# Loading group 0, the weights and half of group 1 as one series of cast DMAs

## The chip, the cores and the metric

The kernel runs on one core of a Trainium2 chip. The metric is the device time of one execution in microseconds (us). A profiled execution adds a trace; its span is the time from the first to the last instruction. Engines are named as in the profile: PE (TensorE matmul), PEld (weight load), DVE (VectorE), ACT (ScalarE), POOL (GpSimd), SP (SyncE).

Every run is labelled fast unless it is more than 1.5% above the fastest run of the same kernel.

## The reference

```python
# x: (8, 4224, 192); weight: (8, 7); w_in: (192, 1024); A_log: (512,); w_out: (512, 192), all float32
w = softmax(weight)                      # 8 heads of 24 channels, 7 taps
x = causal_conv(x, w)                    # out[s] = sum_k w[h, k] * x[s - 6 + k], zero before each sequence
proj = x @ w_in
val, gate = proj[..., :512], proj[..., 512:]
h = exp(A_log)[0] * h + val[:, t]        # scan over the 4224 positions of each sequence
out = (silu(gate) * h) @ w_out
```

## The kernel before

The 33,792 rows are two streams of 16,896, worked side by side. A group is 16 tiles of 96 rows per stream, a quarter is 4 tiles. The conv is a matmul against a banded matrix `tb`; its output is transposed (by PE for the first half of group 0, by the DMA crossbar afterwards) into `xc`. A step projects 512 positions of each stream for one of 4 channel blocks: `pv` (values, scanned on VectorE) and `pg` (gates, SiLU on ScalarE), then GpSimd multiplies. From step 9 on, output matmuls run as well.

The head of the program, shortened and with comments added:

```python
WARM, WARM2 = 8, 6
...
ws = ...; nc.sync.dma_start(ws, weight.unsqueeze(0))
for st in range(2):                       # quarter 0, fp32, cast later on an engine
    load_raw((nc.scalar, nc.sync)[st], 0, st, 0)
nc.gpsimd.dma_start(al, moe_A_log.rearrange("(c p) -> p c", p=P))
for st in range(2):                       # quarter 1, cast in the DMA
    load_cast(0, st, QT, HT)
nc.sync.dma_start(w1r, moe_w_in[0:D1, :]) # fp32 weights, cast on GpSimd
for m in range(0, D2, DI):
    for st in range(2):
        nc.sync.dma_start(w2r[st * D2R : st * D2R + D2R, m : m + DI], moe_w_in[D1:D, m : m + DI])
...
warm(pw, WARM)                            # matmuls on zeros
...                                       # softmax and banded matrix
warm(pw, WARM2)
...
for st in range(2):
    cast_raw((nc.scalar, nc.gpsimd)[st], 0, st)
for st in range(2):
    load_cast(0, st, HT, HT + QT)         # quarter 2
```

w_in has 192 rows; `w1` holds the first 128. `w2` holds the last 64 twice, on partitions 0 to 63 and 64 to 127, one copy for each stream. The start of the pipeline and the first steps:

```python
conv_main(None, pair(ps_g, "pg"), 0, True)    # quarter 0
conv_main(None, pair(ps_v, "pv"), 1, True)    # quarter 1
...
warm(misc()[:, 0:N], 4)
for m in range(0, D2, DI):
    nc.gpsimd.tensor_copy(w1[:, m : m + DI], w1r[:, m : m + DI])
    nc.gpsimd.tensor_copy(w2[:, m : m + DI], w2r[:, m : m + DI])
for st in range(2):
    load_cast(0, st, HT + QT, GT)             # quarter 3
load_cast(1, 0, 0, HT)
trans_pe(0)
phase(-1)                                     # first projection
conv_main(nc.scalar, misc(), 2); trans_main(2)
for s in range(NSTEP):
    ...                                       # scan(s), phase(s), mul(nc.gpsimd, s)
    if gr == 0:
        ...
        if s < 3:
            load_cast(1, (s + 1) % 2, (s + 1) // 2 * HT, (s + 1) // 2 * HT + HT)
        if s == 3:
            nc.gpsimd.dma_start(wout, ...)
        if s in (5, 7):
            load_raw(nc.sync, 2, s // 7)
        if s in (6, 8):
            load_cast(2, s // 8, QT, GT)      # 504 KB each
    ...
    if s in todo:                             # 5, 6, 7, 8, 10, 12, ...: conv and crossbar transpose
        conv(todo[s])
```

At step 7 the mixed channels of group 1 (`ymix`) are convolved; their crossbar transpose is issued on SP at the end of that stretch, and step 11 needs it for its last projection matmuls.

## Time and profile before

| | before |
|---|---|
| time, the first 3 runs | 343.25 to 345.82 us, median 345.59 |
| span of the profiled run | 343.5 us |
| first scan | 17.62 us |
| scan of step 2 / 8 / 12 / 20 | 22.34 / 36.17 / 45.54 / 64.95 us |
| transpose of ymix for step 11 | issued 38.32, landed 6.4 us later, PE waited 0.2 us |

The lines behind this are in the prediction. The waits list puts down a wait to what came last, and gives total, count and longest.

### The profile page before, as it was taken

How to read it: one execution, taken by the hardware profiler on the slowest of the kernel's cores; microseconds unless marked ns; L12 is line 12 of the kernel's file. 1: busy time of each engine (PE TensorE's matmuls, PEld its weight loads, DVE VectorE, ACT ScalarE, POOL GpSimd, SP SyncE). 2: the span in 40 equal slices, each digit the busy share in tenths (PEclk: the TensorE clock that was granted, in tenths of full speed). 3: DMA queues.
4: the chain of work that ended last, by engine and by line, in shares of the span. 5: the costliest groups of instructions: out<-in, count | busy, mean ns of one | idle time of the engine just before them, and what ended most of it. 6: DMA issues, size and time to landing. Idle time of an engine off the chain costs nothing.

```text
span 343.5 us, 7220 instructions
## 1 busy us (share of the span) xinstructions
PE 330.3 (96%) x2604; PEld 179.2 (52%) x2605; DVE 324.3 (94%) x311; ACT 271.1 (79%) x431; POOL 305.8 (89%) x176
## 2 busy tenths in 40 slices
PE   6698999999999999999999999999999999999994
PEld 2433455555545555555545555455555555556444
DVE  3399999999999999999999999999999999999994
ACT  4367888978987888798888789789888888777663
POOL 7569999999989998998998999899899988888882
PEclk9899999999999999999999999999999999999999
DMA  8959999998998999999799799989979954545235
GB/s 190 143 66 183 157 190 248 200 168 203 167 221 145 160 169 239 165 192 188 181 213 149 184 167 158 231 185 176 196 176 168 209 138 126 139 105 149 92 112 169
DMA packets 126839, 58.53 MB, mean 170 GB/s; under 512 B 84338, under 2 KB 126290, under 8 KB 126802
## 3 DMA queue, kind: packets, MB, share of 16 engines
q1 hardware_dynamic: 94722, 45.64, 66.1%
q0 software_dynamic: 31472, 11.90, 31.8%
q10 hardware_dynamic: 608, 0.53, 0.5%
q8 instruction: 20, 0.33, 0.4%
q14 instruction: 17, 0.14, 0.2%
HBM read 31.70 MB, written 25.95 MB: 168 GB/s over the span
## 4 chain that ended last, share of the span: by engine, by line
PE 87%; DVE 4%; DMA 4%; issue 1%; ACT 1%; POOL 0%; DVEq 0%; POOLq 0%; ACTq 0%
PE pm L444 26%; PE pv L361 15%; PE pg L361 15%; PE pg L369 11%; PE pm L257 9%; PE pv L369 8%; DVE h L411 4%; DMA xb<-in_x_dram 3%; DMA xc<-ymix 2%; ACT sg L393 1%; PE pv L257 1%; PE pm L178 1%; PE pg L444 0%; PE pv L444 0%; POOL al L156 0%
## 5 line engine op out<-in xcount | busy, mean ns | idle before, releaser
L411 DVE TENSOR_TENSOR_SCAN h<-av,h,pv 128x512 bf16<-128x512 f32 (+3 forms) x256 | 294.9, 1210 | 2.9 <-issue 1.9
L429 POOL TENSOR_TENSOR y<-sg,h 128x1024 bf16<-128x1024 bf16 x130 | 273.3, 2124 | 27.0 <-ACT sg L393 25.7
L393 ACT ACTIVATE sg<-pg 128x512 bf16<-128x512 f32 x262 | 142.2, 594 | 30.9 <-PE pg L369 29.5
L444 PEld LDWEIGHTS <-y 128*128 128x128 bf16 x1056 | 83.9, 98 | 26.8 <-issue 26.8
L444 PE MATMUL pm<-wout,y 128*128 128x192 bf16 x1024 | 95.6, 247 | 0.0
L361 PE MATMUL pv<-xc,w 128*128 128x512 bf16 x265 | 80.5, 379 | 2.4 <-DVE h L411 2.2
L361 PE MATMUL pg<-xc,w 128*128 128x512 bf16 x262 | 78.3, 378 | 0.3
L468 ACT COPY osb<-pm 128x768 f32<-128x768 f32 x64 | 51.3, 802 | 24.7 <-ACT sg L393 23.2
L361 PEld LDWEIGHTS <-w 128*128 128x128 bf16 x528 | 46.9, 98 | 37.0 <-issue 7.1
L369 PE MATMUL pg<-xc,w 64*128 64x512 bf16 x262 | 51.1, 386 | 0.0
L369 PE MATMUL pv<-xc,w 64*128 64x512 bf16 x266 | 50.5, 376 | 0.2 <-DMA xc<-ymix 0.2
L257 PEld LDWEIGHTS <-tb 112*96 112x96 bf16 x440 | 32.8, 124 | 31.4 <-issue 28.8
L369 PEld LDWEIGHTS <-w 64*128 64x128 bf16 x528 | 15.3, 94 | 57.9 <-issue 57.9
L105 ACT CAST ymain<-pm 96x1024 bf16<-96x1024 f32 x42 | 42.3, 1007 | 1.0 <-PE pm L257 0.8
L257 PE MATMUL pm<-xb,tb 112*96 112x192 bf16 (+2 forms) x420 | 41.4, 237 | 0.0
L121 POOL DMA_DIRECT2D xb<-in_x_dram x28 | 25.3, 905 | 0.0
L411 DVE TENSOR_TENSOR_SCAN h<-av,pv 128x512 bf16<-128x512 f32 (+3 forms) x32 | 24.9, 795 | 0.4 <-PE pv L369 0.4
L105 ACT CAST ymix<-pm 96x1024 bf16<-96x1024 f32 x20 | 20.1, 1007 | 0.0
L105 ACT CAST xb<-xraw 112x768 bf16<-112x768 f32 x19 | 15.8, 833 | 0.0
L178 PE MATMUL pg<-wm 128*128 128x512 bf16 x14 | 5.1, 524 | 1.7 <-DVE wm L171 1.7
L178 PEld LDWEIGHTS <-wm 128*128 128x128 bf16 x18 | 2.1, 129 | 4.4 <-issue 2.2
L257 PE MATMUL pv<-xb,tb 112*96 112x192 bf16 (+2 forms) x13 | 1.9, 327 | 2.2 <-DMA xb<-in_x_dram 2.2
(61 smaller groups left out, 38.7 us busy)
## 6 DMA issues: line engine op xcount, KB each, us to landing
out_dram<-osb SPq DMA_DIRECT2D x65, 384.0 KB, 3.6
xb<-in_x_dram POOLq DMA_DIRECT2D x18, 504.0 KB, 8.8
xraw<-in_x_dram SPq DMA_DIRECT2D x18, 336.0 KB, 4.1
xb<-in_x_dram POOLq DMA_DIRECT2D x4, 336.0 KB, 6.1
xc<-ymain SPq DMA_TRANSPOSE x84, 4.7
xb<-in_x_dram POOLq DMA_DIRECT2D x6, 168.0 KB, 5.7
w1r<-in_moe_w_in_dram SPq DMA_DIRECT2D x1, 512.0 KB, 6.2
w2r<-in_moe_w_in_dram SPq DMA_DIRECT2D x4, 128.0 KB, 6.9
```

Source lines behind the costliest of these rows:

```text
L105: eng.copy(o, i)
L121: eng.dma_start(t[:, b0 : a1 - a0, :], dataclasses.replace(xf, offset=xf.offset + (row + b0 * M) * D, ap=[[D, K], [M * D, a1 - a0 - b0], [ ...
L178: nc.tensor.matmul(ps, wm[:, 0:P], wm, start=True, stop=True)
L257: nc.tensor.matmul(pc[:, :, :, lo - lo0 : hi - lo0], tb[:, h, :], xbs[g][:, :, a : a + QT, lo:hi], start=(lo == lo0), stop=(hi == hi0), sk ...
L361: nc.tensor.matmul(ps[st], w1[:, m * P : (m + 1) * P], xc[:, st, t], start=True, stop=False)
L369: nc.tensor.matmul(ps[st], w2[r, m * P : (m + 1) * P], xc[r, 2, t], start=False, stop=True)
L393: nc.scalar.activation(sg[:, st * N : st * N + N], pgs[st], Act.Silu)
L411: nc.vector.tensor_tensor_scan(h[:, o + lo : o + hi], av[:, c : c + 1].to_broadcast([P, hi - lo]), pv[st][:, lo:hi], initial=0.0 if lo in ...
L429: eng.tensor_mul(y, sg, h)
L444: nc.tensor.matmul(pk[b // 2][:, b % 2, :], y[:, b : N : NB] if w >= NOUT - 2 else y[:, b * P : b * P + P], wout[:, c, :], start=(b % 2 == ...
L468: nc.scalar.copy(osb.rearrange("p (k b) d -> p k (b d)", k=2), po)
```

## The change

The intent was to bring everything that the start needs in order of need, through one queue, with the cast done by the DMA, and to have no such load in flight while the first crossbar transposes run. Core of the diff, shortened and with comments added:

```diff
-WARM = 8
-WARM2 = 6
+WARM = 6
+WARM2 = 4
...
+    x0 = singles.tile([K, D], FP32, name="x0")       # the very first tile, cast on VectorE
+    nc.scalar.dma_start(x0[HB:K, :], xf[0:M, :])
+    nc.sync.dma_start(al, moe_A_log.rearrange("(c p) -> p c", p=P))
     for st in range(2):
-        load_raw((nc.scalar, nc.sync)[st], 0, st, 0)
-    nc.gpsimd.dma_start(al, ...)
-    ...                                              # w1r, w2r: fp32 loads on SP
+        load_cast(0, st, 0, QT)
...
+    for st in range(2):
+        load_cast(0, st, QT, HT)
+    nc.gpsimd.dma_start(w1, moe_w_in[0:D1, :])
+    nc.gpsimd.dma_start(
+        w2,
+        dataclasses.replace(
+            moe_w_in, offset=moe_w_in.offset + D1 * D2, ap=[[0, 2], [D2, D2R], [1, D2]]
+        ),
+    )
...
+    for q in (2, 3):
+        for st in range(2):
+            load_cast(0, st, q * QT, q * QT + QT)
+    for st in range(2):
+        load_cast(1, st, 0, HT)
...
-    warm(misc()[:, 0:N], 4)
-    ...                                              # four weight casts on GpSimd, later loads
+    warm(misc()[:, 0:N], 2)
...
-            if s < 3:
-                load_cast(1, ...)
-            if s == 3:
+            if s in (3, 4):
+                load_cast(1, s - 3, HT, GT)
+            if s == 5:
                 nc.gpsimd.dma_start(wout, ...)
```

Here `ap` lists (step, count) pairs: the source of w2 starts with a pair of step 0, so it reads the 64 rows twice.

More of the change, by code (lines that the diff above doesn't have):

```diff
@@ L115, in load @@
         row = st * TS + (g * GT + a0) * M - HB
-        b0 = 0
-        if g == 0 and a0 == 0:
-            nc.vector.memset(t[0:HB, 0, :], 0.0)
-            eng.dma_start(t[HB:K, 0, :], xf[row + HB : row + K, :])
-            b0 = 1
+        b0 = 1 if row < 0 else 0
         eng.dma_start(
@@ L152 @@
     nc.sync.dma_start(ws, weight.unsqueeze(0))
+    x0 = singles.tile([K, D], FP32, name="x0")
+    nc.scalar.dma_start(x0[HB:K, :], xf[0:M, :])
+    al = singles.tile([P, NC], FP32, name="al")
+    nc.sync.dma_start(al, moe_A_log.rearrange("(c p) -> p c", p=P))
     for st in range(2):
-        load_raw((nc.scalar, nc.sync)[st], 0, st, 0)
-    al = singles.tile([P, NC], FP32, name="al")
-    nc.gpsimd.dma_start(al, moe_A_log.rearrange("(c p) -> p c", p=P))
-    for st in range(2):
-        load_cast(0, st, QT, HT)
-    w1 = singles.tile([P, D2], BF16, name="w1")
-    w2 = singles.tile([P, D2], BF16, name="w2")
-    w1r = singles.tile([P, D2], FP32, name="w1r")
-    w2r = singles.tile([P, D2], FP32, name="w2r")
-    nc.sync.dma_start(w1r, moe_w_in[0:D1, :])
-    for m in range(0, D2, DI):
-        for st in range(2):
-            nc.sync.dma_start(
-                w2r[st * D2R : st * D2R + D2R, m : m + DI], moe_w_in[D1:D, m : m + DI]
-            )
+        load_cast(0, st, 0, QT)
+    nc.vector.memset(x0[0:HB, :], 0.0)
     wm = singles.tile([P, N], BF16, name="wm")
@@ L198 @@
         )
+    for st in range(2):
+        load_cast(0, st, QT, HT)
+    w1 = singles.tile([P, D2], BF16, name="w1")
+    w2 = singles.tile([P, D2], BF16, name="w2")
+    nc.gpsimd.dma_start(w1, moe_w_in[0:D1, :])
[5 more added lines that the diff above has]
+    )
     ident = singles.tile([M, M], BF16, name="ident")
     make_identity(nc, ident)
+    for q in (2, 3):
[3 more added lines that the diff above has]
+        load_cast(1, st, 0, HT)
     wmax = singles.tile([1, H], FP32, name="wmax")
@@ L240 @@
     nc.scalar.activation(quiet, av[:, 0:1], Act.Silu)
-    for st in range(2):
-        cast_raw((nc.scalar, nc.gpsimd)[st], 0, st)
-    for st in range(2):
-        load_cast(0, st, HT, HT + QT)
+    nc.vector.tensor_copy(xbs[0][:, 0, 0, :], x0)
+    zero_halos(0, 0)
     ymain = {}
@@ L490 @@
         )
-    warm(misc()[:, 0:N], 4)
-    for m in range(0, D2, DI):
-        nc.gpsimd.tensor_copy(w1[:, m : m + DI], w1r[:, m : m + DI])
-        nc.gpsimd.tensor_copy(w2[:, m : m + DI], w2r[:, m : m + DI])
-    for st in range(2):
-        load_cast(0, st, HT + QT, GT)
-    load_cast(1, 0, 0, HT)
+    warm(misc()[:, 0:N], 2)
     trans_pe(0)
@@ L535 @@
                 trans_main(3)
-            if s < 3:
-                load_cast(1, (s + 1) % 2, (s + 1) // 2 * HT, (s + 1) // 2 * HT + HT)
-            if s == 3:
+            if s in (3, 4):
+                load_cast(1, s - 3, HT, GT)
+            if s == 5:
                 nc.gpsimd.dma_start(wout, moe_w_out.rearrange("(c p) m -> p c m", p=P))
```

## The prediction

> **What bounds the kernel now.** I read the page first, then the chain of waits, then the busy time by stretch, then the DMA windows of the first 45 us. The page's busy row and first chain row:
>
> ```profile
> PE 330.3 (96%) x2604; PEld 179.2 (52%) x2605; DVE 324.3 (94%) x311; ACT 271.1 (79%) x431; POOL 305.8 (89%) x176
> PE 87%; DVE 4%; DMA 4%; issue 1%; ACT 1%; POOL 0%; DVEq 0%; POOLq 0%; ACTq 0%
> ```
>
> PE and VectorE are both nearly full, so most of the span is closed to this change, which touches loads of the first two groups only. The chain in order of time shows the head:
>
> ```profile
> 3.02 8.75 DMA xb<-in_x_dram
> 11.77 0.04 issue
> 11.81 1.85 PE pv L257 x13
> 13.66 1.72 PE pm L178 x4
> 15.38 0.04 issue
> 15.42 0.50 PE pm L324 x8
> 15.92 0.68 PE pg L324 x16
> 16.60 0.58 PE pv L361 x2
> 17.19 0.37 PE pv L369 x2
> 17.56 0.01 DVEq L411
> 17.57 0.05 issue
> 17.62 4.55 DVE h L411 x4
> ```
>
> Columns are start, length, what. The load of quarter 1 of group 0 (issued at 3.02) lands at 11.77; then 13 conv matmuls, 4 warm-up matmuls, the PE transposes and the first projection follow, and the first scan starts at 17.62. From there two stages follow. In steps 0 to 8 VectorE is the bound: by stretch, it is busy 22.28 of the 22.28 us from 17.62 to 39.90, PE only 19.84, and the waits list has PE waiting 2.2 us for scans. From step 9, when the output matmuls join, PE is back to back: 16 output matmuls begin every 4.82 us (45.20, 50.02, 54.84), that is every two steps, against four scans of 1.2 us. So **the time of the first scan, plus any later stall that exceeds the small slack, is what the change can move**; 345.6 us is the reference.
>
> The DMA stage table of the head:
>
> ```profile
> 5.20:8.58 3.38, 1.94 (x14) 0.93 (x13) 1.04 (x2) 2.16 (x4) 2.39 (x4) 1.00 1.12 273
> 8.58:12.00 3.42, 0.82 (x9) 0.70 (x10) 0.69 (x1) 0.83 (x2) 1.96 (x4) 1.00 1.43 216
> 12.00:15.40 3.40, 3.37 (x17) 2.05 (x16) 1.37 (x2) 1.16 (x2) 2.38 (x4) 0.50 0.72 75
> ```
>
> After the stretch come its length, the busy times of PE, PEld, DVE, ACT and POOL, the granted clock, the DMA share and GB/s. The reader is to see two things: the DMA engines are full (1.12, 1.43) while PE waits, and the stretch after the idle one runs PE at clock 0.50. That is why 13 matmuls take 1.85 us and each warm-up matmul 0.43.
>
> **What the Trainium skill says.** (1) "DMA: Bandwidth & Descriptors", section "Issuing engines are not separate DMA queues": loads from all issuers share the same 16 DMA engines and interleave. The trace agrees: quarter 1 took 8.7 us while 1.0 MB of weights were moved beside it; the same size took 3.6 and 3.8 us from about 12 us on. (2) Same page, "Rules for kernel authors": a leading zero-stride broadcast of c copies confines a DMA to at most c engines; the page also names an exception in which a GpSimd direct copy keeps 16. The new load of w2 has just this source (2 copies of 64 rows). No run here shows which holds. (3) "TensorE: Matmul & The Clock Gate", Part 1: the clock is set from activity in free-running windows of about 3.41 us. The trace agrees (0.50 for 3.4 us after 0.82 us of work in the window before).
>
> **The change part by part.**
>
> Removed: the fp32 staging of group 0's first quarter (648 KB over two hardware queues), 1.0 MB of fp32 weights in flight beside quarter 1, six casts (0.82 on POOL, 0.82 on ACT, 4 x 0.61 on POOL), the 0.95 us POOL issue of A_log, and 2 + 2 + 2 warm-up matmuls. Of the last only the third pair lies on the chain: 2 x 0.43 at half clock, 2 x 0.25 at full.
>
> Added: casts inside the DMA, a 192-column copy on VectorE (under 0.3 us, beside the load) and a small ScalarE memzero.
>
> Moved: the first cast DMA issues at about 1.4, each issue 0.70. Quarter 0: two issues, to 2.8; band mask, 0.8 to 3.6; quarter 1, to 5.0; w1 and w2, to about 6.5; quarters 2 and 3 and half of group 1, to about 11.5 (0.70 for a quarter, 0.86 for a half).
>
> How fast does this series flow? Between 10.5 and 12 us the DMA window counts 746 cast rows of 768 B in 1.5 us, 498 rows per us. Quarters 0 and 1 are 784 + 896 = 1,680 rows, so 3.4 us of flow. The start is slower: packets begin 0.6 us after the end of an issue, and from 24 us, after one, some 1.3 us run at 50 instead of 190 GB/s; I allow 1 us for that and 0.8 us more because A_log's first packets of this queue came later still (4.0, issue ended 2.31). Last row of quarter 1: 2.1 + 0.6 + 1.8 + 3.4 = 7.9; landing about 0.9 later (the 336 KB load at 22.56: its 896th row is counted at about 27.0, it landed at 27.66; others 1.1), so **8.8 instead of 11.77**. Quarter 0 lands near 7, ready about when the mask product, the copy and the memzero are.
>
> From landing to first scan: 13 matmuls at full clock 1.2 (7 took 0.63 at 8.93), two warm-ups 0.5, then 15.42 to 17.62 unchanged, 2.2: first scan at 12.7. At half clock it is 1.85 + 0.86 + 2.2, 13.7. I take 13.0, a gain of **4.6 us**. The weights must be there by 11.7 and 12.2: w1 and w2 are 512 KB each at about 370 GB/s (the window 5.5 to 6.5, nearly all w1, moved 368), 1.4 us each, so their data end at 9.3 and 10.7 and land by 11.6 if w2 uses 16 engines: just in time.
>
> Given back later (T0 is the first scan):
> - Quarter 2 follows the weights: 896 rows, 1.8 us, lands at about 13.5. PE wants it right after the first projection (before: 17.46, T0 - 0.2). PE waits some 0.8 us; slack before scan 1 was about 0.35. Loss 0.5.
> - The second half of group 1 is issued after multiplies 3 and 4 instead of 1 and 2. Before, its last load was issued at 28.44 (T0 + 10.8) and landed 7.7 later (T0 + 18.5); the conv that reads it ran at 37.58 (T0 + 20.0). Now multiplies come every 2.34 us from T0 + 2.9, so the last issue starts at T0 + 14.4; landing after 5.1 to 7.7 is T0 + 19.5 to 22.1. Loss 0 to 2, say 1.1.
> - wout issues at about T0 + 17.5 instead of T0 + 13.8; with 6.5 us to land, T0 + 24.0, and the first output matmul ran at T0 + 22.3; with the delay above it wants it at T0 + 23.4. The crossbar transpose of ymix (38.32, 6.44 us, PE waited 0.23 us for it) may meet these loads as well. Loss 0.6.
>
> Sum: -4.6 + 0.5 + 1.1 + 0.6 = -2.4; 345.6 - 2.4 = 343.2. I say **343.0**.
>
> **The rivals.**
>
> A. w2 on two engines. For: the page's rule fits the access pattern word for word. Against: the exception; and the author trimmed the warm-ups, which looks like tuning on a measured head. Then 64 rows of 4 KB per engine at 159 to 175 ns (the 4,096 B packets of w1r; the window from 5.5 has 92 packets in 95% of 16 engine-us, 165 ns) take 10.5 us, w2 lands near 19.5 and T0 is about 20.5 to 21; quarter 2 waits behind it on these two engines. Time 350. I give it 20%.
>
> B. The gain stays whole: later loads land in time because nothing else is in flight. Time 341.
>
> C. New stalls at steps 8 to 11 eat everything: the late half of group 1, wout, the staged load of group 2 and transposes meet there, and PE, the bound from step 9 on, cannot recover. Time 345 to 346.
>
> D. The head was not limited by DMA but by the mask chain on ACT and VectorE: quarter 0's conv ran at 8.93 behind an ACT cast that sat behind a 1.28 us table load. That cast goes, so against; at worst quarter 1's conv begins near 9.5 and the time is 344.
>
> **Range and chances.** Without A I expect 340 to 346; A gives 348 to 352. Range 339.5 to 349.0. Over 2% faster needs 338.7, a first scan at 10.7 with no new stall, before the weights can land: 3%. Over 2% slower needs 352.5, A plus further stalls: 3%. Within 2%: 94%.
>
> **What would show it.** First scan near 13 (12.3 to 14) in the chain; quarter 1 landing near 8.8; granted clock 1.00 from the conv of quarter 1 to the scan; w2 landing at 11 to 12.5 (near 19 or 20 would show A); a PE wait under 1.5 us at the conv of quarter 6 and at the first output matmul; the period of 4.82 us unchanged afterwards. It is wrong if w2 lags, if POOL's issue blocks on a full series of descriptors, or if the first crossbar transposes, issued near 15.5 with group 1 still loading, land later than step 3 needs them (T0 + 9).

## The result and the profile after

The changed kernel took 358.54 us (median of 4 runs, 356.99 to 359.40), against 345.70 for the kernel before in the same rounds (343.25 to 347.93). The ratio is 1.037, with a 95% interval of 1.029 to 1.045: slower by 3.7%. A ratio is the mean time of one kernel's fast runs over that of the other's of the same rounds, so it is not quite the ratio of the medians. The range of the prediction ended at 349.0.

The milestones of the two profiled runs (spans 343.5 and 357.6 us), as starts of scans:

| us | before | after | difference |
|---|---|---|---|
| first scan | 17.62 | 21.20 | 3.58 |
| step 2 | 22.34 | 29.18 | 6.84 |
| step 8 | 36.17 | 43.01 | 6.84 |
| step 11 | 43.20 | 50.04 | 6.84 |
| step 12 | 45.54 | 56.42 | 10.88 |
| step 16 | 55.31 | 69.04 | 13.73 |
| step 20 | 64.95 | 78.69 | 13.74 |

So there are **two separate losses**: 6.84 us before step 2, and 6.89 us between steps 11 and 16. Up to step 20 everything else runs at the old pace; 0.4 us of the 14.1 come later. The timeline of the changed kernel shows the first (L260 is the conv matmul, L364 and L372 are the full and the 64-row projection matmuls, L414 the scan; brackets give the idle time before and what ended it):

```profile
9.49 1.99 PE L260 MATMUL pv<-xb,tb 112*96 112x192 bf16 x13 [1.50 <-DMA xb<-in_x_dram]
...
14.12 0.69 PE L364 MATMUL pv<-xc,w 128*128 128x512 bf16 x2
...
20.49 0.60 PE L372 MATMUL pv<-xc,w 64*128 64x512 bf16 x2 [5.67 <-DMA w<-in_moe_w_in_dram]
21.20 2.33 DVE L414 TENSOR_TENSOR_SCAN h<-av,pv 128x512 bf16<-128x512 f32 x2 [6.26 <-PE pv L372]
```

Quarter 1 was there at 9.5 instead of 11.8 and the first projection began at 14.12 instead of 16.60. The head did get faster, and then PE stood for 5.67 us waiting for w2. The DMA traffic between 18 and 20 us says why:

```profile
DMA packets 26, 0.05 MB, mean 27 GB/s; under 512 B 0, under 2 KB 0, under 8 KB 26
q0 software_dynamic: 26, 0.05, 14.1%
```

The cast queue is q0; its packets took 14.1% of the time of 16 engines, about two engines' worth, and moved 27 GB/s, while nothing else was in flight. Up to here the other engines had brought quarters 2 and 3 and group 1 past it. What remained of those behind w2 then trickled in at the same width:

```profile
q0 software_dynamic: 380, 0.14, 19.9%
```

That is 380 rows from 20.5 to 26.5 us, 63 per us. The kernel before moved 746 rows in 1.5 us, 497 per us (the prediction wrote 498); 63 is an eighth of that, as two engines are of 16. The chain shows the consequence for quarter 2, and further down the second loss:

```profile
7.88 14.40 DMA xb<-in_x_dram
22.28 0.14 issue
22.42 1.08 PE pm L260 x7
...
44.32 0.77 ACT sg L396 x2
45.09 10.60 DMA xc<-ymix
55.69 0.04 issue
55.74 0.61 PE pv L372 x2
56.34 2.67 PE pm L447 x16
```

The same place in the kernel before:

```profile
38.32 6.44 DMA xc<-ymix
44.77 0.04 issue
44.81 0.39 PE pv L369 x2
45.20 1.43 PE pm L444 x16
```

The transpose of ymix took 10.6 us to land instead of 6.4, and the 16 output matmuls after it took 2.67 us instead of 1.43, because PE came back at half clock. By stretch (length, then busy times of PE, PEld, DVE, ACT, POOL, then clock, DMA share, GB/s):

```profile
45.09:55.74 10.65, 6.34 (x51) 3.18 (x49) 7.38 (x7) 7.60 (x12) 10.63 (x7) 0.96 1.35 144
55.74:63.70 7.96, 7.96 (x41) 4.05 (x41) 4.37 (x4) 2.83 (x5) 2.23 (x2) 0.63 1.22 226
```

By the milestones the wait makes up 4.04 us of the second loss and the slow stretch after it 2.85.

One trap: the stretch view gives a clock of 1.00 for the head of the changed kernel, but its 7 conv matmuls at 6.91 took 1.09 us and the 13 at 9.49 took 1.99; the kernel before did 7 in 0.63. The trace has no clock record before 13.84 us in this run, and the view then shows 1.00. Matmul durations are the safer witness.

### The profile page after: what moved, and what is told of

The parts are those of the page before. It is cut to its first block, busy times and chain, and to the rows that moved or that the text cites.

```text
span 357.6 us, 7193 instructions
## 1 busy us (share of the span) xinstructions
PE 335.5 (94%) x2599; PEld 181.8 (51%) x2599; DVE 324.7 (91%) x311; ACT 270.7 (76%) x431; POOL 305.0 (85%) x174
## 4 chain that ended last, share of the span: by engine, by line
PE 84%; DMA 7%; DVE 3%; POOL 2%; issue 1%; ACT 1%; DVEq 0%; POOLq 0%; ACTq 0%
PE pm L447 25%; PE pv L364 15%; PE pg L364 15%; PE pg L372 11%; PE pm L260 9%; PE pv L372 8%; DMA xb<-in_x_dram 4%; DMA xc<-ymix 3%; DVE h L414 3%; POOL xb L117 1%; ACT sg L396 1%; PE pg L447 0%; PE pv L447 0%; POOL w L193 0%; DVE osb L107 0%
## 5 line engine op out<-in xcount | busy, mean ns | idle before, releaser
L414 DVE TENSOR_TENSOR_SCAN h<-av,h,pv 128x512 bf16<-128x512 f32 (+3 forms) x256 | 295.0, 1211 | 9.4 <-issue 8.4
L447 PEld LDWEIGHTS <-y 128*128 128x128 bf16 x1056 | 84.9, 99 | 27.1 <-issue 27.0
L447 PE MATMUL pm<-wout,y 128*128 128x192 bf16 x1024 | 96.8, 248 | 0.0
L364 PE MATMUL pv<-xc,w 128*128 128x512 bf16 x266 | 81.8, 385 | 1.9 <-DVE h L414 1.9
L364 PE MATMUL pg<-xc,w 128*128 128x512 bf16 x262 | 79.3, 382 | 0.3
L364 PEld LDWEIGHTS <-w 128*128 128x128 bf16 x528 | 47.6, 99 | 37.0 <-issue 7.6
L372 PE MATMUL pv<-xc,w 64*128 64x512 bf16 x266 | 51.4, 383 | 10.0 <-DMA w<-in_moe_w_in_dram 5.7
L372 PE MATMUL pg<-xc,w 64*128 64x512 bf16 x262 | 51.5, 389 | 0.0
L260 PEld LDWEIGHTS <-tb 112*96 112x96 bf16 x440 | 33.8, 127 | 32.3 <-issue 29.7
L372 PEld LDWEIGHTS <-w 64*128 64x128 bf16 x528 | 15.2, 94 | 68.4 <-issue 62.1
L260 PE MATMUL pm<-xb,tb 112*96 112x192 bf16 (+2 forms) x420 | 42.1, 240 | 1.6 <-DMA xb<-in_x_dram 1.6
L414 DVE TENSOR_TENSOR_SCAN h<-av,pv 128x512 bf16<-128x512 f32 (+3 forms) x32 | 25.1, 797 | 8.9 <-PE pv L372 8.9
L117 POOL DMA_DIRECT2D xb<-in_x_dram x30 | 26.9, 899 | 0.8 <-POOLq L586 0.8
L105 ACT CAST xb<-xraw 112x768 bf16<-112x768 f32 x18 | 15.0, 833 | 0.0
L260 PE MATMUL pv<-xb,tb 112*96 112x192 bf16 (+2 forms) x13 | 2.0, 341 | 1.5 <-DMA xb<-in_x_dram 1.5
```

The lines of the kernel that those rows point to most:

```text
L105: eng.copy(o, i)
L117: eng.dma_start(t[:, b0 : a1 - a0, :], dataclasses.replace(xf, offset=xf.offset + (row + b0 * M) * D, ap=[[D, K], [M * D, a1 - a0 - b0], [ ...
L260: nc.tensor.matmul(pc[:, :, :, lo - lo0 : hi - lo0], tb[:, h, :], xbs[g][:, :, a : a + QT, lo:hi], start=(lo == lo0), stop=(hi == hi0), sk ...
L364: nc.tensor.matmul(ps[st], w1[:, m * P : (m + 1) * P], xc[:, st, t], start=True, stop=False)
L372: nc.tensor.matmul(ps[st], w2[r, m * P : (m + 1) * P], xc[r, 2, t], start=False, stop=True)
L414: nc.vector.tensor_tensor_scan(h[:, o + lo : o + hi], av[:, c : c + 1].to_broadcast([P, hi - lo]), pv[st][:, lo:hi], initial=0.0 if lo in ...
```

## The experiments

Theory after the result: (a) w2 was confined to two DMA engines; (b) the late loads of group 1 and wout met the transposes before step 11. Rivals: (b) merely follows from (a), or the long series of cast DMAs is slow in itself.

### e1: w2 by two DMAs

```diff
-    nc.gpsimd.dma_start(w2, dataclasses.replace(moe_w_in, ..., ap=[[0, 2], [D2, D2R], [1, D2]]))
+    for st in range(2):
+        nc.gpsimd.dma_start(w2[st * D2R : st * D2R + D2R, :], moe_w_in[D1:D, :])
```

> The changed kernel with one edit: w2 comes by two cast DMAs of 64 partitions each instead of one DMA whose source is a zero-stride pair. Theory: the pair confined the transfer to two DMA engines (w2 landed near 20.4 us and everything queued behind it on those two engines until 27 us), which cost 6.8 us up to step 2. Then w2 lands before 13.5, the first scan starts at 12.8 to 14, the scan of step 2 near 19 instead of 29.18. The second stall (PE waiting 4.3 us for the transpose of ymix at step 11, and half clock after it) has a cause of its own, the late loads of group 1 and wout, and stays: about 348 us. Rival 1: the second stall only follows from the first; then it goes as well and the time is about 341. Rival 2: the series of cast DMAs is slow in itself; w2 still lands after 18 and the time stays near 358.

Median 348.96 us (20 runs, 343.19 to 351.65); the kernel before in the same rounds 347.18 (34 runs, 343.04 to 350.93). The ratio of fast runs is 0.996 (0.992 to 1.000), but it counts only 6 of the 20 runs; by the medians of all runs it is 0.5% slower. So some 9.6 us of the loss went with the source pattern of one DMA (358.54 less 348.96, from different rounds). In the profile the first scan came at 16.38 and step 2 at 22.25, 6.9 us before the changed kernel, where the kernel before has 22.34. (a) is confirmed, the slow series is not: w2 no longer holds anything up. The second loss stayed, on its own:

```profile
9.81 2.00 PE pv L256 x13
...
38.16 11.09 DMA xc<-ymix
49.29 0.39 PE pv L368 x2
49.68 2.33 PE pm L443 x16
```

The first scan was expected at 12.8 to 14. It was later because PE ran at half clock until 19.3 us (13 matmuls in 2.00 us). The profiled run (351.65 us) is one of those labelled slow; e3 and e6 below show the same wait at step 11 in runs labelled fast.

### e2: group 1 and wout loaded early

```diff
-            if s in (3, 4):
-                load_cast(1, s - 3, HT, GT)
-            if s == 5:
+            if s in (1, 2):
+                load_cast(1, s - 1, HT, GT)
+            if s == 3:
                 nc.gpsimd.dma_start(wout, ...)
```

> The changed kernel with one edit: the second half of group 1 is loaded at steps 1 and 2 and wout at step 3, as early as before, instead of steps 3, 4 and 5. Theory of two causes: the first scan stays at 21.2 and step 2 at 29.2, but the cast loads no longer meet the transposes of group 1, the wait of 4.3 us at step 11 falls under 1 us and the clock stays at 1.00 there: about 351.5 us. Rival 1 (the second stall follows from the first): no change, 358.

Median 358.20 us (4 runs), as the changed kernel. The transpose of ymix took 9.4 us and PE waited 3.1 us. **Part (b) of my theory fell**: the late loads of group 1 are not what delays that transpose.

### e3: both edits

> Both edits: w2 by two cast DMAs, and the second half of group 1 and wout loaded at steps 1 to 3. Theory: neither stall, first scan near 13, then the pace of the kernel before: 341 us (345.7 less 4.6). Rival 2 (a slow series): near 351. Rival 3: without the first stall the loads of group 1 meet the first crossbar transposes, which then come late for step 3: 343 to 346.

Median 349.18 us (15 runs), ratio 1.010 (1.007 to 1.012). First scan at 15.60, and a wait of 3.2 us at step 11 again. This run also bears on the intent: with the second half of group 1 loaded at steps 1 and 2, the transpose issued at 25.90 took 7.4 us, where e1 with its late loads has 2.4 for the transpose at 27.83. So keeping cast loads away from the first transposes does make them quick; what it was worth here is small, as PE waited only 0.3 us for that transpose in e3.

### e4: the pair on the hardware queue

The kernel before, with one edit: its four fp32 loads of w2 become one on SP with the same pair as source.

> The kernel before with one edit: its four fp32 loads of w2 become one load on the hardware queue with the same zero-stride pair as source. Theory: the pair confines this transfer to two engines as well, 64 rows of 4 KB per engine at 0.16 to 0.17 us, so w2 lands 10 to 11 us after it starts, near 16, the cast and the loads behind it on POOL slip by 4 us, and the time is 349 to 352. Rival: only cast DMAs suffer, time 345 to 346.

Median 356.37 us (4 runs), ratio 1.028 (1.022 to 1.033). The chain and, from 12 to 20 us, the queue:

```profile
2.58 18.60 DMA w2r<-in_moe_w_in_dram
21.18 0.05 issue
21.23 0.62 POOL w L495
```

```profile
q1 hardware_dynamic: 82, 0.34, 11.0%
```

82 packets of 4 KB in 8 us are again about two engines' worth (12.5% would be two of 16). The pair confines a plain DMA on the hardware queue as it does a cast DMA. It lost 9 us rather than the 3 to 6 expected. By the scan of step 8 (42.91) the profile is 6.74 us behind the kernel before: GpSimd waited 11.3 us for w2 and could not issue the loads behind it. Another 4.0 us went between the scans of steps 11 and 16, where PE waited 2.6 us for the transpose of ymix and came back at half clock: the second loss appears here too.

### e5: the kernel before

> The kernel before, unchanged, for a second profile: its times in the last rounds ran from 343.0 to 350.9, so the first profile (343.5) may be a fortunate one. Theory: the wait for the transpose of ymix at step 11 (0.23 us in the first profile, with 6.4 us to landing) is itself of varying length in the kernel before, and a run near the median of 347.2 shows 2 to 4 us of it. Rival: the stall is of the changed kernels alone; then the wait stays under 0.5 us.

346.11 us, one run. The wait at step 11 was 0.3 us and the transpose landed after 6.5 us. The rival held: neither of the two profiles of the kernel before has the long wait. The first scan was at 18.61, as PE stayed at half clock until 17.27 us in this run, a full us later than in the first profile with nothing changed.

### e6: the warm-up of the kernel before

```diff
-WARM = 6
-WARM2 = 4
+WARM = 8
+WARM2 = 6
...
-    warm(misc()[:, 0:N], 2)
+    warm(misc()[:, 0:N], 4)
```

This is on top of e1.

> e1 (w2 by two DMAs) with the warm-up matmuls of the kernel before (8, 6 and 4 instead of 6, 4 and 2). In e1 PE ran at half clock until 19.3 us, so that quarter 1's conv, the transposes and the first projection took 6.6 us from landing to first scan instead of 3.9. Theory: the shorter warm-up is the reason; here the full clock comes before 9 us, the first scan is at 13.5 to 14.5 and the time 2 us below e1: about 346.5. Rival: the clock depends on the phase of free-running windows more than on 4 matmuls; then no difference that can be told (348 to 349).

Median 347.81 us (20 runs), ratio 1.002 (0.999 to 1.004); e1 had 348.96. The profiled run was still at half clock until 14.18 us, and its first scan came at 16.23. So the number of warm-up matmuls alone does not decide when the clock rises. The median is 1.2 us lower than e1's, in other rounds: too little to call the shorter warm-up shown as a cause.

### e7: the kernel before, group 2 loaded later

Now I looked at what lay beside the transpose in all profiles. Just before or after it, GpSimd issues the first 504 KB cast load of group 2.

```diff
-            if s in (6, 8):
-                load_cast(2, s // 8, QT, GT)
+            if s in (9, 10):
+                load_cast(2, s - 9, QT, GT)
```

> The kernel before with the two 504 KB cast loads of group 2 issued at steps 9 and 10 instead of 6 and 8. Theory: these loads are what the transposes of group 1 meet just before step 11; without them the ymix transpose lands within 5 us, the wait at step 11 is gone in each run, the time falls to 343 to 344 with a smaller spread. Rival: the transposes are slow for another reason (the staged load and the store on the same queue); then nothing changes, 347.

Median 352.37 us (4 runs), ratio 1.013 (1.006 to 1.020): slower clear of noise. The transpose landed after 5.4 us and PE no longer waited for it, as expected. But now the load was late. The chain:

```profile
47.55 14.53 DMA xb<-in_x_dram
```

PE waited 5.2 us for it at the conv of step 16. I had moved the load too far.

### e8: all three

e6 with the late group 2 loads of e7.

> e6 with the group 2 loads at steps 9 and 10: w2 by two DMAs, the full warm-up, no cast load beside the transposes that step 11 needs. Theory: first scan at 13.5 to 14.5 and no stall at step 11, so 3.5 us below e7: about 340. If the stall at step 11 has another reason: 346, as e6.

Median 343.93 us (10 runs), ratio 0.993 (0.990 to 0.997). First scan at 13.56; the transpose of ymix landed after 5.6 us; group 2 was late here too (PE waited 1.9 us at step 16). The full clock came at 5.42 us in this run, with the same warm-up as e6.

### What the profiles have in common

Issue times of the two DMAs in each profiled run so far, and what became of the transpose:

| run | ymix transpose issued | group 2 load issued | load minus transpose | landing | PE wait |
|---|---|---|---|---|---|
| before | 38.32 | 38.46 | +0.14 | 6.4 | 0.2 |
| e5 | 39.25 | 39.48 | +0.23 | 6.5 | 0.3 |
| e7 | 38.02 | 44.47 | +6.45 | 5.4 | none |
| e8 | 35.13 | 41.03 | +5.90 | 5.6 | none |
| after | 45.09 | 44.74 | -0.35 | 10.6 | 4.3 |
| e1 | 38.16 | 37.81 | -0.35 | 11.1 | 4.6 |
| e2 | 44.49 | 43.97 | -0.52 | 9.4 | 3.1 |
| e3 | 36.23 | 35.56 | -0.67 | 9.5 | 3.2 |
| e4 | 44.99 | 43.60 | -1.39 | 8.9 | 2.6 |
| e6 | 36.86 | 36.50 | -0.36 | 9.4 | 2.7 |

The issue of the load, before and after, as the timeline has it:

```profile
38.46 1.00 POOL L121 DMA_DIRECT2D xb<-in_x_dram  x1
44.74 1.00 POOL L117 DMA_DIRECT2D xb<-in_x_dram  x1
```

Half a microsecond separates the two classes. New theory: it is the **order of these two issues** that decides. The change had turned it: from the start of the scan of step 8, the transpose is issued 2.15 us later before and 2.08 after, but the cast load 2.29 before and 1.73 after. GpSimd has one issue of 0.86 us fewer to do in steps 0 to 5 (three instead of four), so its back-to-back multiplies reach the load earlier (from the second multiply to this load GpSimd has no idle time in either profile). Three runs test the order; a fourth adds warm-ups.

### e9: e6 with the order mended

```diff
-            if s in (6, 8):
-                load_cast(2, s // 8, QT, GT)
+            if s in (7, 8):
+                load_cast(2, s - 7, QT, GT)
```

> e6 (w2 by two DMAs, full warm-up) with the group 2 loads at steps 7 and 8 instead of 6 and 8, so that the first follows the ymix transpose of step 8 instead of preceding it. Theory: what decides the landing of that transpose is whether the cast load was issued just before it (six profiles: 8.9 to 11.1 us) or after it (four profiles: 5.4 to 6.5). Here it lands in 5 to 7 us, PE waits under 0.7 us at step 11, and the load is not late for step 14: 342 to 344, a little under e8. Rival: the length depends on how full the DMA engines are, not on the order: it lands in 9 us again, time 347 to 348.

Median 342.61 us (4 runs, 341.30 to 344.15), ratio 0.987 (0.981 to 0.993). The load followed by 2.1 us, the transpose landed after 5.0 us and PE did not wait for it:

```profile
DMA to landing us min/median/max: 5.0/5.0/5.0
```

The first scan came at 13.12. PE still waited 1.4 us for quarter 2 and 1.6 us for the second half of group 1. The ratio is clear of noise, but under the 2% of a verdict.

### e10: the changed kernel with the order mended

The same edit alone, w2 still as a pair.

> The changed kernel with this one edit (group 2 loads at steps 7 and 8), w2 still as a pair. Theory of the order: the first stall stays (first scan at 21.2), the second goes: 358.4 less 4.3 us of wait and 2 to 3 us of half clock after it, 351 to 352. Rival: 357 to 358.

Median 352.55 us (4 runs), ratio 1.016 (1.010 to 1.021), against 358.54 for the changed kernel. First scan at 21.88; the transpose landed after 5.5 us and PE waited 0.5 us:

```profile
PE pv L372 <- DMA w<-in_moe_w_in_dram: 5.3, 1, 5.3
PE pv L372 <- DMA xc<-ymix: 0.5, 1, 0.5
```

The second loss is gone but for 0.8 us by step 20, and the first untouched (step 2 at 30.30): each can be had without the other.

### e11: the kernel before with the order turned

```diff
-            if s in (6, 8):
+            if s in (5, 8):
                 load_cast(2, s // 8, QT, GT)
```

> The kernel before with its first group 2 load one step earlier (steps 5 and 8 instead of 6 and 8), so that it precedes the ymix transpose of step 8 by 1.5 to 2 us. Theory of the order: that transpose lands in 9 to 11 us instead of 6.4, PE waits 2.5 to 4.5 us at step 11, half clock may follow, the time rises by 3 to 6 us to 350 to 353. Rival (the changed head is needed for the stall): no change, 347.

Median 349.51 us (20 runs, 346.29 to 352.31), against 346.58 for the kernel before (35 runs). The load was issued 1.87 us ahead of the transpose, which took 8.7 us; PE waited 2.4 us:

```profile
PE pv L369 <- DMA xc<-ymix: 2.4, 1, 2.4
```

The changed head is not needed for this stall. The ratio of fast runs is 1.006 (1.004 to 1.009), but it leaves out the slowest 4 of the 20; by the medians it is 0.8%. The effect is at the low end of what I expected, since no half clock followed in the profiled run. One limit: e9, e10 and e11 each moved the load by 2.0 to 2.5 us against the transpose. That half a microsecond is enough rests on the profiles of the table, not on an edit.

### e12: four more warm-up matmuls

e9 with `warm(misc()[:, 0:N], 4)` between the convs of quarters 0 and 1.

> e9 with four more warm-up matmuls between the conv of quarter 0 and that of quarter 1, where PE sits idle for 0.4 to 1.5 us. Theory: the full clock then comes in the head whatever the phase of the windows, first scan at 13.4 to 14 in each run: 341 to 342 with a small spread. Rival: the extra matmuls delay quarter 1's conv as much as the clock gives: same as e9.

Median 342.95 us (16 runs, all but one within 341.88 to 343.82), ratio 0.990 (0.987 to 0.992). First scan at 13.71, full clock from 5.07 us. It is not faster than e9 in the median; whether it makes the clock more reliable can't be told from 4 runs of e9.

## Why the prediction was wrong

**What bounds the kernel: right.** The prediction said that only the time of the first scan and later stalls can move the end. The milestones bear that out: outside two stretches the difference stays constant to 0.01 us up to step 20.

**The series of loads: right for what precedes w2.** GpSimd's issues ended at 11.61 (11.5 foretold); quarter 1 landed at 9.4 (8.8).

**The failing step: "by 11.6 if w2 uses 16 engines: just in time".** w2 used two engines and landed 14.7 us after its issue, at 20.4. The prediction had this as rival A, with the right mechanism, the right size (w2 near 19.5, first scan at 20.5 to 21, measured 21.20), and a chance of 20%. The rule fitted the access pattern word for word, and no run of the kernel before had a DMA that could have argued against it. The evidence on the other side was a guess at the author's intent from trimmed warm-ups. A stated rule that matches should have carried the central estimate, near 350.

**The aftermath of A was under-sized.** "quarter 2 waits behind it on these two engines" is what happened, but the prediction gave A's time as 350. e10 has this loss alone and takes 352.55. In the profile of the changed kernel 6.84 us had been lost by step 2, 3.26 of them after the first scan. And the stated range, up to 349.0, left out most of the 348 to 352 that the prediction gave to A.

**The second loss was a term mis-sized and a trigger misplaced.** "The crossbar transpose of ymix ... may meet these loads as well. Loss 0.6" covered wout and the transpose together. The wait and the half clock after it were 6.9 us. And "these loads" named group 1 and wout; e2 shows that moving them back changes nothing. The load that matters is the first one of group 2, which the change does not touch; it only came 0.5 us earlier against the transpose. e9, e10 and e11 show that the order decides, in both directions. Rival C ("New stalls at steps 8 to 11") had the place, but let them cost no more than the gain of 4.6 us.

**The clock: half right.** The warm-ups were counted only as PE time saved (0.5 to 0.9 us), and the 13 conv matmuls as 1.2 us at full clock, 1.85 at half. In the changed kernel they took 1.99. What the shorter warm-up contributes is not settled: with 6, 4 and 2 the full clock came at 19.29 (e1) or came early and was lost again from 8.09 to 14.91 (e3); the changed kernel, e2 and e10 had it at 13.84, 12.76 and 15.50 and lost it again while PE waited for w2; with 8, 6 and 4 it came at 14.18 (e6), 5.42 (e8), 4.46 (e9), and in the kernel before at 5.17 and 17.27.

**The gain that was foretold exists.** With w2 split, the order mended and the warm-ups of the kernel before (e9), the first scan is at 13.12 (13.0 foretold), quarter 2 costs a PE wait of 1.4 us (0.8 foretold) and the late half of group 1 one of 1.6 us (a loss of 1.1 foretold), and e9 takes 342.61 us (343.0 foretold). The agreement of the totals is partly luck: in its rounds e9 was 4.0 us under the kernel before by the medians, in the profiles 2.2 us by step 20, where a gain of 2.6 was foretold, and both waits were longer than foretold. One reason is a slip: the time of the last issue, T0 + 14.4, leaves out the 0.86 us of the issue just before it. With it the same reckoning gives about T0 + 15.0, and e9 has T0 + 16.0. So the rest of the sum was right in size, not term by term; and it does not mend the prediction, which was for a kernel that has both faults.

**What stays open.** How the DMA engines come to serve a transpose so much later when a cast load has been issued 0.4 us earlier: the trace here does not say which packet ran on which engine. What the traces do show is that the first transpose issued after that load landed within 0.7 us of the load itself in 11 of the 14 profiles. In the kernel before this is the next transpose, of ymain: issued at 39.80, it landed at 46.39, the load at 46.05. In most profiles, then, a transpose behind the load comes with it, early or late (here after 6.6 us). Also open is why the clock rises early in some executions and late in others.

## What to carry to other kernels

Before merging DMAs, look at the slowest dimension of both access patterns: a two-fold repeat as the outermost source dimension turned a 512 KB load into one of 27 GB/s and held up everything queued behind it. When a queue's issues are moved, check not only when each lands but which neighbour it now overtakes; here taking one 0.86 us issue away let an untouched load slip ahead of a transpose, which cost as much as the first fault. And after a PE stall of a few microseconds, allow for a stretch at half clock: it followed the waits of 3.1 us and more at steps 11 and 16 (after, e1, e2, e3, e7); of the shorter ones it followed those of 2.6 us (e4) and 1.9 us (e8), but not those of 2.7 us (e6) and 2.4 us (e11).

## What the Trainium skill lacked or had wrong

- "DMA: Bandwidth & Descriptors", section "Rules for kernel authors": the rule on a zero-stride repeat outermost was right, for a cast DMA from GpSimd (26 packets in 2 us, 14.1% of 16 engines) and for a plain one from SP (82 packets in 8 us, 11.0%). The page's exception for "some direct copies" from GpSimd does not say which; this one was not among them. It gives no figure for what the later loads on the same queue lose: here 63 rows per us instead of 497.
- The same section says that a transpose next to ordinary DMAs "needs nothing". As to correctness no run contradicts it. As to time, the crossbar transpose of ymix landed after 5.0 to 6.5 us when a 504 KB cast load was issued after it (before, e5, e7 to e10, e12) and after 8.7 to 11.1 us when the load was issued first (after, e1 to e4, e6, e11). No page gives such times.
- "TensorE: Matmul & The Clock Gate", Part 1, gives one busy window of about 3.4 us as enough for the full clock. In e6 PE is shown busy for 3.42 of the 3.42 us from 3.94 to 7.36 (window edges counted back from the clock record at 14.18), yet the 7 conv matmuls at 8.61 took 1.08 us, half speed. Seven of the matmuls in that window use one partition only; whether that matters no run here shows.
